# First expert's number from batch 0's routing, made inside the last attention step, with first-layer pieces in place of fillers

## The chip, the cores and the metric

One core of one Trainium2 chip runs the whole program. The metric is the device time of one execution in microseconds. Its engines work side by side, each through its own list of instructions in order: PE (matmuls, with PEld for the loads of weights), DVE, ACT and POOL (elementwise work and reductions), and SP, which only issues transfers here. An instruction that has to wait holds all that stand behind it in its engine's list.

## What is computed

Attention in two steps for 4 batches with 8 heads (576 positions, 64 channels, 32 packed queries `p`), then two mixture-of-experts layers with 8 experts.

```python
def sm_attn(qq, kk, vv):
    s = scale * np.matmul(qq, kk.transpose(0, 1, 3, 2))
    s = s - np.max(s, axis=-1, keepdims=True)
    a = np.exp(s)
    a = a / (np.sum(a, axis=-1, keepdims=True) + 1e-09)
    return np.matmul(a, vv)
p_packed = sm_attn(p, k, v)
out = sm_attn(q, p_packed, p_packed)

# first layer: x is [2304, 512]
logits = x @ w_gate
expert_idx = np.argmax(logits, axis=1)
...
h = np.maximum(np.einsum('ecd,edf->ecf', disp, w1), 0.0)   # the tokens kept for each expert
y = np.einsum('ecf,efd->ecd', h, w2)
out[i] = gate_w[i] * y[expert_idx[i], pos[i]]
# second layer: the same with its own weights, no capacity, and a second gate
```

All tokens of a batch go to one expert with these inputs. The kernel finds that expert on the chip, fetches its weights alone, and keeps a general path for other inputs, which is not run here.

## The kernel before

**Attention.** The loop over the batches is a pipeline written out by hand. `att_iter(b)` does the first scores of batch b, the packed values of b - 1 and the second softmax of b - 2, head groups 0 and 1 apart. `att_last` is the step of the last batch (n = 3, o = 2, r = 1), `att_end` what is left behind it (o = 3, r = 2, z = 1); the second softmax of batch 3 follows behind `att_end`. In the names of instructions: `tp` and `a1Tp` are transposes on PE, `T` and `a1T`, `a1L` their copies out of PSUM; `s` are scores; `nb` is the row maximum of the first softmax, `a` its exponential on ACT; `pp` is the packed value, `pps`, `ppTp` and `ppT` its scaled form, transpose and copy; `sT` is the second score, whose softmax goes DVE (`mx`, maximum), POOL (subtract), ACT (exponential), DVE (`dn`, one over the sum), POOL (multiply), DVE (L401, back to `a2T`).

**Routing of batch 0.** `g1_t(0, 1)` gives batch 0's logits `Lall` on DVE (L434). `ga` and `ga2` make the one-hot of the maximum: `mx`, `d`, `first`, `mx`, `oh` (L166 to L176). `gb` ranks the tokens on PE (`rk`), `gc` turns ranks into `kp` and `K`, the tokens within capacity (L465 to L470), `gd` counts `K` on PE (`cp`) and takes the expert with most tokens (`primary`, L205 to L212). L222 turns it into an integer, `e_i`. SP loads it into a register (L685) and uses it as the address of the weights: `moe1_load1` (eight transfers of 256 KB, L516) and `moe1_load2` (four of 512 KB, L529).

**First expert layer of batch 0.** Its matmuls are made of a high and a low half of each operand. `moe1_x` splits the input: `xh` on ACT (L538), `xl` on POOL (L539). The layer is cut into twelve pieces in the list `fill`: four `ppw` pieces (the packed values times a quarter of the weights, then `wh` on ACT and `wl` on DVE) and eight `h` pieces (twelve matmuls each, then ACT's high half L573 and DVE's low half L580). `FL(n)` places the next n of them wherever it stands. `att_end` has five places, each for one piece, and one `warm(4)`, four matmuls on zeros whose result nobody reads. The other seven pieces stand behind, among the second softmax of batch 3. Then the second-layer weights are split (`w2ah` on ACT, `w2al` on DVE, L498), and `y`, the second layer, begins. Inside the first `y` stands `lp`, the routing of batches 1 to 3, which needs the last `a2T`.

**PSUM.** All PE results share four buffers of PSUM (`psm`). A matmul that starts a new tile waits until the reader of the tile that held the buffer is done.

Of the kernel before, what the change touches and what calls it, by code (L numbers as in the profile page):

```python
# [11 lines left out]
I32 = mybir.dt.int32  # L12
ACTF = mybir.ActivationFunctionType
ALU = mybir.AluOpType
AX = mybir.AxisListType
# [13 lines left out]
def tile_kernel(  # L29
# [16 lines left out]
    nc = tc.nc  # L46
# [112 lines left out]
    def bc(ap, n):  # L159
        return ap.unsqueeze(2).to_broadcast([ap.shape[0], ap.shape[1], n])  # L160

    def onehot(L, nm, V=nc.vector):

        n = L.shape[1]
        mx = sm_p.tile([128, n], FP32, tag=nm + "mx", name="mx")
        nc.vector.tensor_reduce(mx, L, axis=AX.X, op=ALU.max)  # L166
        d = sm_p.tile([128, n, E], FP32, tag=nm + "d", name="d")
        V.tensor_tensor(d, L, bc(mx, E), op=ALU.subtract)
        first = sm_p.tile([128, n, E], FP32, tag=nm + "f", name="first")
        rv = revv.rearrange("p b t e -> p (b t) e")[:, 0:n, :]  # L170

        def rest():
            nc.vector.scalar_tensor_tensor(first, d, 0.0, rv, op0=ALU.is_equal, op1=ALU.mult)
            nc.vector.tensor_reduce(mx, first, axis=AX.X, op=ALU.max)
            oh = sm_p.tile([128, n, E], BF16, tag=nm + "oh", name="oh")
            nc.vector.tensor_tensor(  # L176
                oh, rev.unsqueeze(1).to_broadcast([128, n, E]), bc(mx, E), op=ALU.is_equal)
            return oh, d
        return rest

    def denom(ex, nm):
# [38 lines left out]
    def to_int(src, nm, V=nc.vector):  # L220
        t = keep_p.tile(list(src.shape), I32, name=nm)
        V.tensor_copy(t, src)  # L222
        return t
# [48 lines left out]
    def transp(b, nm, G, eng=0):  # L272

        src = raws.pop((nm, b, G))
        t = t_p.tile([128, J, 128], FP32, tag="T", name="T")
        for j0, n in ((0, 6), (6, 3)):
            ps = psm("tp")
            for j in range(n):
                tr(nc, ps[:, j // 3, (j % 3) * 128:(j % 3) * 128 + 128],
                   src[:, 2 * (j0 + j):2 * (j0 + j) + 2, :].rearrange("p r d -> p (r d)"), ident)  # L280
            evac(eng, t[:, j0:j0 + n, :].rearrange("x (u j) c -> x u (j c)", j=3), ps[:, 0:n // 3, 0:384])
        T[nm, b, G] = t
# [96 lines left out]
    def s2_max(b, G):  # L379
        mx = as_p.tile([128, 2 * NB2], FP32, tag=f"mx2{G}", name="mx2")  # L380
        nc.vector.tensor_reduce(mx, sv(b, G), axis=AX.X, op=ALU.max)
        at["mx", b, G] = mx
# [44 lines left out]
    def g1_t(b0, b1):  # L427
        tp = psm("lt")
        for j in range(3):
            tr(nc, tp[:, 0, j * 128:(j + 1) * 128], lgT[:, j * 128:(j + 1) * 128], ident)  # L430
        tv = tp[:, 0, 0:384].rearrange("p (j u g b e) -> p b j u e g", j=3, u=2, g=2, b=4)
        for b in range(b0, b1):
            for u, t in ((0, 0), (1, 2)):
                nc.vector.tensor_reduce(  # L434
                    Lall[:, b, t:t + 2 + u, :], tv[:, (b - 1) % 4, 0:2 + u, u], axis=AX.X, op=ALU.add)

    def ga(b0, b1, nm, V=nc.vector):
        L = Lall[:, b0:b1].rearrange("p b t e -> p (b t) e")
# [96 lines left out]
    def moe1_x(a2, lo_eng):  # L535
        xh = xs_p.tile([128, 2, S], FP32R, tag="xh", name="xh")
        xl = xs_p.tile([128, 2, S], FP32R, tag="xl", name="xl")
        nc.scalar.activation(out=xh, in_=a2, func=ACTF.Copy)  # L538
        lo_eng.tensor_tensor(xl, a2, xh.bitcast(FP32), op=ALU.subtract)  # L539
        return xh, xl  # L540
# [143 lines left out]
    def val(ap, hi):  # L684
        return nc.values_load(ap, engines=sp, min_val=0, max_val=hi)  # L685
# [184 lines left out]
    def warm(n):  # L870
        ps = psm("warm")
        for _ in range(n):
            mm(nc, ps[:, 0, 0:256], wz[:, 0:128], wz, True, True)

    with tc.manual_schedule():
# [56 lines left out]
        def att_last():  # L932

            n, o, r = B - 1, B - 2, B - 3
            a1_T(o, 0, 0)
            s2_max(r, 0)
            s2_sub(r, 0, nc.gpsimd)
            s1_mm(n, 0)
            g1_t(0, 1)
            transp(o, "q", 0)  # L940
            s2_max(r, 1)
            s2_sub(r, 1, nc.gpsimd)
            s1_max(n, 0)
            s1_exp(n, 0)
            a1_T(o, 1, 1)
            s2_exp(r, 0)
            pp_mm(o, 0)
            s1_mm(n, 1)
            s1_max(n, 1)
            rest = ga(0, 1, "a0", nc.gpsimd)  # L950
            s1_exp(n, 1)
            pp_mm(o, 1)
            pp_scale(o)
            ga2(0, rest, nc.gpsimd)
            transp(o, "q", 1)
            s2_exp(r, 1)
            pp_T(o)
            gb(0, 1)
            gc(0, 1, "a0")
            s2_sum(r, 0)  # L960
            s2_mul(r, 0, nc.gpsimd)
            a1_T(n, 0, 0)
            s2_mm(o, 0)
            g1_g(o)
            s2_tr(o, 0)
            st["rest0"] = gd(0, 1, "a0")
            st["e0"] = to_int(pe1[:, 0:1], "e0_i")
            s1_rs(n)
            s2_mm(o, 1)
            s2_back(r, 0)  # L970
            s2_tr(o, 1)
            st["h"] = new_h()
            st["x"] = moe1_x(a2T[:, 0], nc.gpsimd)

        def att_end():

            o, r, z = B - 1, B - 2, B - 3
            transp(o, "q", 0)
            s2_sum(z, 1)
            s2_mul(z, 1, nc.gpsimd)  # L980
            a1_T(o, 1, 0)
            pp_mm(o, 0)
            s2_max(r, 0)
            pp_mm(o, 1)
            s2_sub(r, 0, nc.gpsimd)
            transp(o, "q", 1)
            pp_scale(o)
            s2_exp(r, 0)
            warm(4)
            pp_T(o)  # L990
            s2_back(z, 1)
            s2_max(r, 1)
            FL()
            s2_sub(r, 1, nc.gpsimd)
            s2_exp(r, 1)
            s2_mm(o, 0)
            s2_tr(o, 0)
            s2_sum(r, 0)
            g1_g(o)
            FL()  # L1000
            s2_mul(r, 0, nc.gpsimd)
            FL()
            s2_back(r, 0)
            s2_sum(r, 1)
            s2_mul(r, 1, nc.gpsimd)
            FL()
            s2_mm(o, 1)
            s2_tr(o, 1)
            s2_back(r, 1)
            FL()  # L1010
# [19 lines left out]
        for b in range(B):  # L1030
# [12 lines left out]
                att_iter(b)  # L1043
            else:
                att_last()
        e0 = val(st["e0"][0:1, 0:1], E - 1)
        st["w1"] = moe1_load1(e0)
        w2s = moe1_load2(e0)


        for i in range(4):
# [179 lines left out]
```

## Time and profile before

| | |
|---|---|
| median of 3 runs (lowest to highest) | 271.77 us (270.22 to 272.42) |
| the profiled execution: its time, its span | 269.92 us, 268.2 us |
| busy in the span | PE 250.5, PEld 215.8, DVE 131.0, ACT 100.2, POOL 35.0 us |
| mean granted clock of PE | 0.976 |

The span is the time from the first to the last instruction of the profiled execution. The busy time is the sum over an engine's instructions; an engine that is busy for a small share of the span can still be the one that others wait for in one stretch of it. The granted clock is the share of full speed (2.4 GHz) that PE got; 0.50 is 1.2 GHz.

### The profile page before, as it was taken

Reading aid. Unit: us, or ns where it says so; the run is one execution under the profiler, and the core shown is the slowest. Engines: PE = TensorE matmul, PEld = TensorE weight load, DVE = VectorE, ACT = ScalarE, POOL = GpSimd, SP = SyncE. Lnnn points to the kernel's source line nnn. Section 1 sums busy time; section 2 is a strip of 40 time slices with the busy share of each in tenths; the row PEclk is TensorE's granted clock in tenths of the full one; section 3 lists DMA queues with packets and bytes.
Section 4 is the critical chain, followed back from the end, with each engine's and each line's share of the span. In section 5 each row is a group of like instructions: output and inputs, shape, how many; then the busy total and the mean of one; then the engine's idle time right before and its main releaser. Section 6 shows DMA issues by size and latency. Waiting matters only on the chain.

```text
span 268.2 us, 5617 instructions
## 1 busy us (share of the span) xinstructions
PE 250.5 (93%) x2281; PEld 215.8 (80%) x2281; DVE 131.0 (49%) x323; ACT 100.2 (37%) x165; POOL 35.0 (13%) x65
## 2 busy tenths in 40 slices
PE   8879989959989989999999999999999999999980
PEld 6647657627886979879999999998888999988860
DVE  0232877985996685278641245695030425611000
ACT  2856566723480410345430243263221414411110
POOL 5001333533350240000000000000020000002000
PEclk9997999977999999999999999999999999999997
DMA  6999999059720004985696034228121460001211
GB/s 243 373 300 282 354 312 298 13 121 213 222 77 2 0 0 158 221 204 185 158 256 227 21 87 129 78 79 233 43 60 42 126 227 2 0 0 43 60 42 48
DMA packets 32867, 37.14 MB, mean 138 GB/s; under 512 B 6336, under 2 KB 27456, under 8 KB 32832
## 3 DMA queue, kind: packets, MB, share of 16 engines
q1 hardware_dynamic: 32832, 36.69, 46.8%
q8 instruction: 20, 0.33, 0.5%
q14 instruction: 15, 0.12, 0.2%
HBM read 31.25 MB, written 4.72 MB: 134 GB/s over the span
## 4 chain that ended last, share of the span: by engine, by line
PE 76%; DVE 9%; DMA 6%; SPq 4%; issue 1%; POOL 1%; ACT 0%; ACTq 0%; DVEq 0%; POOLq 0%
PE h L21 25%; PE o L21 19%; PE y L21 18%; DMA r<-in_q_dram 4%; PE tp L25 3%; PE pp L21 2%; DMA wraw<-in_moe_w_dram 2%; PE s L21 2%; PE l L21 2%; PE lp L21 2%; PE ppw L21 1%; SPq L269 1%; PE a1Tp L25 1%; DVE dn L392 1%; DVE eq L208 1%
## 5 line engine op out<-in xcount | busy, mean ns | idle before, releaser
L21 PE MATMUL o<-w2bh,h 128*128 128x512 f32 x144 | 45.9, 391 | 0.0
L21 PE MATMUL y<-h,w2ah 128*128 128x288 f32 x256 | 44.7, 296 | 0.0
L21 PEld LDWEIGHTS y<-h,w2ah 128*128 128x128 f32 x256 | 37.6, 189 | 0.0
L580 DVE SCALAR_TENSOR_TENSOR h<-h 128x576 fp32r<-128x576 f32 (+3 forms) x64 | 25.8, 447 | 20.7 <-ACT h L573 20.7
L573 ACT ACTIVATE h<-h 128x576 fp32r<-128x576 f32 x32 | 20.4, 650 | 35.9 <-PE h L21 32.3
L21 PEld LDWEIGHTS o<-w2bh,h 128*128 128x128 f32 x144 | 26.9, 188 | 5.7
L21 PE MATMUL o<-w2bl,h 128*128 128x512 f32 x80 | 31.3, 391 | 0.0
L21 PE MATMUL y<-h,w2al 128*128 128x288 f32 x128 | 27.6, 297 | 0.8 <-DVE w2al L498 0.8
L21 PE MATMUL h<-yh,w1bh 128*128 128x288 f32 x128 | 27.5, 296 | 0.0
L21 PE MATMUL h<-yh,w1bl 128*128 128x288 f32 x128 | 27.4, 295 | 0.0
L21 PE MATMUL h<-yl,w1bh 128*128 128x288 f32 x128 | 27.3, 295 | 0.0
L241 ACT ACTIVATE T<-tp 128x768 f32<-128x768 f32 (+1 forms) x32 | 18.9, 650 | 11.4 <-PE tp L25 11.3
L679 POOL TENSOR_SCALAR osb<-osb,g 64x512 f32<-64x512 f32 x2 | 3.1, 1570 | 147.5 <-DVE osb L678 147.5
L21 PEld LDWEIGHTS y<-h,w2al 128*128 128x128 f32 x128 | 20.5, 189 | 1.5 <-DVE w2al L498 1.0
L25 PE MATMUL tp<-ident,r 128*128 128x128 f32 x144 | 19.6, 283 | 2.0 <-DMA r<-in_q_dram 1.9
L25 PEld LDWEIGHTS tp<-ident,r 128*128 128x128 f32 x144 | 16.4, 146 | 5.8 <-issue 2.4
L21 PEld LDWEIGHTS h<-yh,w1bh 128*128 128x128 f32 x128 | 20.6, 189 | 0.2
L21 PEld LDWEIGHTS h<-yh,w1bl 128*128 128x128 f32 x128 | 20.6, 188 | 0.0
L21 PEld LDWEIGHTS h<-yl,w1bh 128*128 128x128 f32 x128 | 20.6, 188 | 0.0
L589 ACT ACTIVATE yh<-y 128x576 fp32r<-128x576 f32 x8 | 5.2, 652 | 39.9 <-PE y L21 39.9
L671 ACT ACTIVATE osb<-o,g 128x512 f32<-128x512 f32 x8 | 5.5, 688 | 36.9 <-PE o L21 29.0
L590 DVE TENSOR_TENSOR yl<-y,yh 128x576 fp32r<-128x576 f32 x8 | 6.0, 755 | 25.7 <-ACT yh L589 25.7
(177 smaller groups left out, 378.3 us busy)
## 6 DMA issues: line engine op xcount, KB each, us to landing
wraw<-in_moe_w_dram SPq DMA_DIRECT2D x24, 512.0 KB, 5.5
r<-in_k_dram SPq DMA_DIRECT2D x8, 576.0 KB, 7.7
r<-in_q_dram SPq DMA_DIRECT2D x8, 576.0 KB, 9.6
v<-in_v_dram SPq DMA_DIRECT2D x8, 512.0 KB, 10.7
wraw<-in_moe_w_dram SPq DMA_DIRECT2D x16, 256.0 KB, 5.4
out_dram<-zt SPq DMA_DIRECT2D x2, 1152.0 KB, 7.6
out_dram<-osb SPq DMA_DIRECT2D x8, 256.0 KB, 2.0
a2s<-a2T SPq DMA_DIRECT2D x1, 576.0 KB, 3.6
```

The source lines that it names most:

```text
L21: return nc.tensor.matmul(out, lhsT=lhsT, rhs=rhs, start=start, stop=stop)
L25: return nc.tensor.transpose(out, in_, ident)
L208: nc.vector.scalar_tensor_tensor(eq, eq, 0.0, revv[0:1, 0, 0:n, :], op0=ALU.is_equal, op1=ALU.mult)
L241: nc.scalar.activation(out=o, in_=i, func=ACTF.Copy)
L269: nc.sync.dma_start(t, src[b, :, 128 * VR:].rearrange("h p d -> p h d"))
L392: nc.vector.tensor_reduce(dn, sv(b, G), axis=AX.X, op=ALU.add)
L573: nc.scalar.activation(out=hi, in_=ps[:, :, 0:HS], func=ACTF.Relu)
L580: nc.vector.scalar_tensor_tensor(o, i, 0.0, a.bitcast(FP32), op0=ALU.max, op1=ALU.subtract)
L589: nc.scalar.activation(out=half(y[0][:, c, :]), in_=ps[:, :, 0:HS], func=ACTF.Copy)
L590: nc.vector.tensor_tensor(half(y[1][:, c, :]), ps[:, :, 0:HS], half(y[0][:, c, :]).bitcast(FP32), op=ALU.subtract)
L671: nc.scalar.activation(out=o[:n], in_=ps[:n, 0, :], func=ACTF.Copy, scale=g2[:n, t:t + 1])
L679: nc.gpsimd.tensor_scalar(o[:n], o[:n], g2[:n, t:t + 1], None, op0=ALU.mult)
```

## The change

Batch 0's one-hot is begun right behind its logits, and the expert's number is taken from it: from the routing of batch 0's first token, not from the count of all. The integer is made there (L943), and the loads of the first-layer weights are issued there. `d` goes from POOL to DVE; `first` and the second `mx` go from the second half of the one-hot to its first half. `moe1_x` moves from the end of `att_last` up to behind `ga2`. `att_end` gets one more place for a piece, and two pieces instead of the four fillers. The second-layer weights are asked for at the same place in the code as before.

```diff
@@ onehot
-        V.tensor_tensor(d, L, bc(mx, E), op=ALU.subtract)
+        nc.vector.tensor_tensor(d, L, bc(mx, E), op=ALU.subtract)
         first = sm_p.tile([128, n, E], FP32, tag=nm + "f", name="first")
         rv = revv.rearrange("p b t e -> p (b t) e")[:, 0:n, :]
+        nc.vector.scalar_tensor_tensor(first, d, 0.0, rv, op0=ALU.is_equal, op1=ALU.mult)
+        nc.vector.tensor_reduce(mx, first, axis=AX.X, op=ALU.max)
 
         def rest():
-            nc.vector.scalar_tensor_tensor(first, d, 0.0, rv, op0=ALU.is_equal, op1=ALU.mult)
-            nc.vector.tensor_reduce(mx, first, axis=AX.X, op=ALU.max)
             oh = sm_p.tile([128, n, E], BF16, tag=nm + "oh", name="oh")
...
+        rest.mx = mx
         return rest
@@ att_last
             g1_t(0, 1)
+            rest = ga(0, 1, "a0")
+            e0_i = keep_p.tile([1, 1], I32, name="e0_i")
+            nc.vector.tensor_scalar(e0_i, rest.mx[0:1, 0:1], -1.0, float(E), op0=ALU.mult, op1=ALU.add)
+            st["e0"] = val(e0_i, E - 1)
+            st["w1"] = moe1_load1(st["e0"])
             transp(o, "q", 0)
...
             s1_max(n, 1)
-            rest = ga(0, 1, "a0", nc.gpsimd)
             s1_exp(n, 1)
             pp_mm(o, 1)
             pp_scale(o)
             ga2(0, rest, nc.gpsimd)
+            st["x"] = moe1_x(a2T[:, 0], nc.gpsimd)
             transp(o, "q", 1)
...
             st["rest0"] = gd(0, 1, "a0")
-            st["e0"] = to_int(pe1[:, 0:1], "e0_i")
...
             st["h"] = new_h()
-            st["x"] = moe1_x(a2T[:, 0], nc.gpsimd)
@@ att_end
             s2_max(r, 0)
+            FL()
             pp_mm(o, 1)
...
             s2_exp(r, 0)
-            warm(4)
+            FL(2)
             pp_T(o)
...
-        e0 = val(st["e0"][0:1, 0:1], E - 1)
-        st["w1"] = moe1_load1(e0)
-        w2s = moe1_load2(e0)
+        w2s = moe1_load2(st["e0"])
```

How the lists of instructions change at three places (line numbers after the change are higher by one from L180 on, and by six or more in `att_last` and behind it).

DVE in `att_last`, from batch 0's logits to the scaling of the packed values, before and then after:

```order
L434 TENSOR_REDUCE Lall<-lt 128x24
L381 TENSOR_REDUCE mx_824<-sT 128x18
L307 TENSOR_REDUCE nb<-s 128x1
L243 COPY a1T<-a1Tp 128x512
L243 COPY a1L<-a1Tp 64x128
L307 TENSOR_REDUCE nb<-s 128x1
L166 TENSOR_REDUCE mx<-Lall 128x5
L350 TENSOR_SCALAR pps<-pp,sm 128x128 x2
L173 SCALAR_TENSOR_TENSOR first<-d,revv 128x40
L174 TENSOR_REDUCE mx<-first 128x5
L176 TENSOR_TENSOR oh<-rev,mx 128x40
```

```order
L435 TENSOR_REDUCE Lall<-lt 128x24
L166 TENSOR_REDUCE mx<-Lall 128x5
L168 TENSOR_TENSOR d<-Lall,mx 128x40
L171 SCALAR_TENSOR_TENSOR first<-d,revv 128x40
L172 TENSOR_REDUCE mx<-first 128x5
L943 TENSOR_SCALAR e_i<-mx 1x1
L382 TENSOR_REDUCE mx_855<-sT 128x18
L308 TENSOR_REDUCE nb<-s 128x1
L244 COPY a1T<-a1Tp 128x512
L244 COPY a1L<-a1Tp 64x128
L308 TENSOR_REDUCE nb<-s 128x1
L351 TENSOR_SCALAR pps<-pp,sm 128x128 x2
```

Five instructions, from `mx` to `e_i`, now stand ahead of the maxima and copies of the softmax.

ACT a little later in `att_last`, before and then after (the first row is the exponential of the second head group):

```order
L314 ACTIVATE a_880,sm<-s,nb 128x9x32x2
L241 ACTIVATE T<-tp 128x768
L241 ACTIVATE T<-tp 128x384
L388 ACTIVATE sT<-sT 128x576
L241 ACTIVATE a1T<-a1Tp 128x512
L241 ACTIVATE a1L<-a1Tp 64x128
L538 ACTIVATE xh<-a2T 128x1152
```

```order
L315 ACTIVATE a_906,sm<-s,nb 128x9x32x2
L539 ACTIVATE xh<-a2T 128x1152
L242 ACTIVATE T<-tp 128x768
L242 ACTIVATE T<-tp 128x384
L389 ACTIVATE sT<-sT 128x576
L242 ACTIVATE a1T<-a1Tp 128x512
L242 ACTIVATE a1L<-a1Tp 64x128
```

`xh` moved ahead of five other instructions; `xl` on POOL waits for it alone. On PE the place of `cp` and of the scores behind it is the same, but the scores now use a PSUM buffer that DVE frees with `gsz` (L414 before), where they waited for PE and ACT:

```order
L21 LDWEIGHTS ones16_89 [waits DVE_49]
L21 MATMUL cp_979<-K16_941,ones16_89 128x40 [waits PE_49]
L21 MATMUL s_995<-T_911,ppT_124 32x288 [waits PE_49,Activation_49]
L21 MATMUL s_995<-T_911,ppT_124 32x288 x7
L25 MATMUL tp_1043<-ident_84,r_548 128x128 [waits DMAHW0_49,DVE_49]
```

```order
L21 LDWEIGHTS ones16_89 [waits DVE_49]
L21 MATMUL cp_1007<-K16_969,ones16_89 128x40 [waits Activation_49]
L21 MATMUL s_1021<-T_939,ppT_124 32x288 [waits DVE_49]
L21 MATMUL s_1021<-T_939,ppT_124 32x288 x7
L25 MATMUL tp_1043<-ident_84,r_548 128x128 [waits DMAHW0_49,Activation_49]
```

DVE at the end of the stretch, in front of the second layer, before and then after:

```order
L556 TENSOR_TENSOR wl<-ppw,wh 128x512
L392 TENSOR_REDUCE dn_1320<-sT 128x18
L393 TENSOR_SCALAR dn_1320<-dn_1320 128x18
L394 RECIPROCAL dn_1320<-dn_1320 128x18
L392 TENSOR_REDUCE dn_1326<-sT 128x18
L393 TENSOR_SCALAR dn_1326<-dn_1326 128x18
L394 RECIPROCAL dn_1326<-dn_1326 128x18
L580 SCALAR_TENSOR_TENSOR h<-h 128x576
L498 TENSOR_TENSOR w2al<-wraw,w2ah 128x1024 x2
L401 STREAM_TRANSPOSE a2T<-sT 128x9x32x2
L580 SCALAR_TENSOR_TENSOR h<-h 128x576 x2
L401 STREAM_TRANSPOSE a2T<-sT 128x9x32x2
```

```order
L382 TENSOR_REDUCE mx_1326<-sT 128x18
L581 SCALAR_TENSOR_TENSOR h<-h 128x576 x2
L393 TENSOR_REDUCE dn_1360<-sT 128x18
L394 TENSOR_SCALAR dn_1360<-dn_1360 128x18
L395 RECIPROCAL dn_1360<-dn_1360 128x18
L393 TENSOR_REDUCE dn_1366<-sT 128x18
L394 TENSOR_SCALAR dn_1366<-dn_1366 128x18
L395 RECIPROCAL dn_1366<-dn_1366 128x18
L581 SCALAR_TENSOR_TENSOR h<-h 128x576
L499 TENSOR_TENSOR w2al<-wraw,w2ah 128x1024 x2
L402 STREAM_TRANSPOSE a2T<-sT 128x9x32x2 x2
```

The last three low halves of `h` stood behind `w2al` (two of them in the rows shown, one just behind); now all eight stand ahead of it.

## Rows read from the trace of the kernel before

**Rows 1.** Busy time by engine, mean granted clock, DMA share, GB/s, three windows.

```profile
core 0: us, PE busy (x) PEld busy (x) DVE busy (x) ACT busy (x) POOL busy (x), PEclk, DMA share, GB/s
42.30:54.30 12.00, 11.68 (x279) 8.77 (x278) 10.91 (x32) 8.68 (x17) 5.85 (x6) 1.00 0.41 112
54.30:66.50 12.20, 8.75 (x94) 5.31 (x92) 8.64 (x19) 4.29 (x7) 4.59 (x4) 0.72 0.86 174
66.50:85.00 18.50, 17.74 (x164) 15.37 (x165) 17.94 (x28) 8.59 (x13) 5.81 (x5) 1.00 0.39 115
```

**Rows 2.** Chain that ended last: start us, us, what (four `h` pieces in the last).

```profile
54.11 0.12 DVE e_i L222
...
57.66 5.12 DMA wraw<-in_moe_w_dram
...
123.68 6.58 PE h L21 x48
```

**Rows 3.** PE in time: start, us, line, operation, xcount [idle before <-releaser].

```profile
49.42 0.72 PE L21 MATMUL s<-T,ppT 64*32 64x288 f32 x16
...
56.12 0.60 PE L21 MATMUL warm<-wz 128*128 128x256 bf16 x4 [1.36 <-DVE sT L371]
58.22 0.66 PE L25 MATMUL ppTp<-ident,pps 128*128 128x128 f32 x2 [1.50 <-DVE pps L350]
59.20 1.85 PE L21 MATMUL ppw<-wraw,ppT 64*32 64x256 f32 x9 [0.33 <-DMA wraw<-in_moe_w_dram]
...
80.29 0.52 PE L21 MATMUL y<-h,w2al 128*128 128x288 f32 x2 [0.76 <-DVE w2al L498]
```

**Rows 4.** Busy time in windows of one microsecond, columns as in rows 1.

```profile
57.00:58.00 1.00, 0.00 (x0) 0.00 (x0) 1.00 (x4) 0.00 (x0) 0.71 (x1) 0.61 0.87 273
...
64.00:65.00 1.00, 1.00 (x8) 1.00 (x9) 0.93 (x5) 0.60 (x1) 0.12 (x1) 0.97 1.12 220
```

**Rows 5.** DVE in time, columns as in rows 3.

```profile
42.09 0.30 DVE L434 TENSOR_REDUCE Lall<-lt 128x16 f32<-128x32 f32 x2 [0.63 <-PE lt L25]
...
45.18 0.76 DVE L307 TENSOR_REDUCE nb<-s 128x1 f32<-128x576 f32 x1 [0.64 <-PE s L21]
...
48.09 0.23 DVE L468 TENSOR_SCALAR kp<-kp,capf 128x5 f32<-128x5 f32 x1
48.36 0.20 DVE L470 TENSOR_TENSOR K<-oh,kp 128x40 bf16<-128x40 bf16 x1
...
49.65 0.12 DVE L414 COPY gsz<-gp 128x16 f32<-128x16 f32 x1
...
51.09 2.60 DVE L208 SCALAR_TENSOR_TENSOR eq<-eq,revv 1x8 f32<-1x8 f32 x1
...
57.12 0.69 DVE L381 TENSOR_REDUCE mx<-sT 128x18 f32<-128x576 f32 x1
...
58.91 0.42 DVE L360 COPY ppT<-ppTp 128x256 f32<-128x256 f32 x1 [0.59 <-PE ppTp L25]
...
62.21 0.69 DVE L556 TENSOR_TENSOR wl<-ppw,wh 128x512 fp32r<-128x512 f32 x1 [1.55 <-ACT wh L555]
...
66.52 0.76 DVE L580 SCALAR_TENSOR_TENSOR h<-h 128x576 fp32r<-128x576 f32 x1 [1.16 <-ACT h L573]
...
78.38 3.00 DVE L498 TENSOR_TENSOR w2al<-wraw,w2ah 128x1024 fp32r<-128x1024 f32 x2
...
81.99 1.38 DVE L580 SCALAR_TENSOR_TENSOR h<-h 128x576 fp32r<-128x576 f32 x2
```

**Rows 6.** ACT and POOL in time, columns as in rows 3.

```profile
46.03 0.80 ACT L314 ACTIVATE a<-s,nb 128x576 f32<-128x576 f32 x1 [0.71 <-DVE nb L307]
...
49.27 1.16 ACT L538 ACTIVATE xh<-a2T 128x1152 fp32r<-128x1152 f32 x1
...
51.00 2.67 POOL L539 TENSOR_TENSOR xl<-a2T,xh 128x1152 fp32r<-128x1152 f32 x1
...
58.40 1.16 POOL L385 TENSOR_TENSOR sT<-sT,mx 128x576 f32<-128x576 f32 x1
```

**Rows 7.** DVE in time, routing of batches 1 to 3, under POOL's `w2al`.

```profile
94.52 2.39 DVE L470 TENSOR_TENSOR K<-oh,kp 128x120 bf16<-128x120 bf16 x1
```

## Prediction

> **What bounds the kernel now.** I read the busy time of the stretch that the change touches first, 42.3 to 85 us, in three windows [rows 1]. PE is nearly full in the first and the last (11.68 of 12.00, 17.74 of 18.50) but has 8.75 of 12.20 in the middle, at a mean granted clock of 0.72. The chain of waits says why: the expert's number e_i is ready at 54.11 + 0.12 = 54.2, and the weights fetched by it are the last thing waited for until 57.66 + 5.12 = 62.8 [rows 2]. PE in order of time shows the hole: waits of 1.36, 1.50 and 0.33 us between 54.8 and 59.2 [rows 3]. One-microsecond windows then show the clock at half (1.2 GHz) from inside 57:58 (0.61, so from about 57.2) to the start of 64:65 (0.97, so to about 64.1) [rows 4]. Waits of 3.2 us and work at half clock: that is what the change fills.
>
> DVE is the other half of the picture. It has 10.91 of 12.00 in the first window and 17.94 of 18.50 in the last [rows 1]. Between them its own idle pieces are 0.59, 1.55 and 1.16, all waits for PE or ACT [rows 5]. At the end of the stretch it is PE that waits: y is held 0.76, until 80.29, by DVE's w2al (low half of the second-layer weights) [rows 3, 5]. So the two engines take turns, and a gain on PE is kept only if DVE gets to w2al earlier too.
>
> **The change, part by part.**
>
> *Weights.* e_i is now made right behind batch 0's logits, which DVE has at 42.09 + 0.30 = 42.4 [rows 5]. Five small DVE instructions that wait for each other, 0.20 to 0.23 each like kp and K [rows 5], some 1.2 in all: e_i at 43.6, 10.6 earlier. From the number to the fourth of the eight transfers it took 8.6 (54.2 to 62.8); that would be 52.2. Attention's own loads are ahead in the queues: DMA is 0.41 busy over 42.3:54.3, 4.9 us, so until about 48 [rows 1]. A transfer of 256 KB at 220 GB/s is 1.2 us [rows 4]: first pair near 51, fourth near 53, last near 58. PE asks for the first pair at 55 or later (below) and for each next one several microseconds after. So the transfers are hidden, by attention's matmuls; a pair that came late would cost its own 2.4.
>
> *The five instructions in front.* They stand ahead of mx, both nb and the copies of a1T. 1.2 late, of which DVE waited 0.64 anyway before the second nb [rows 5], and two of them no longer come later. Left on DVE at the end of this list: +0.3 (bounds 0 and 0.5). PE's second pp waits for a1L and, with it, pps and kp: about +0.5 there.
>
> *xh and xl moved up.* This is the term that decides. xh (1.16 on ACT) now stands right behind the second group's exponential, which started at 46.03 and now starts near 46.4; with 0.80 and its accumulator read it ends near 47.2, xh near 48.4. So POOL's xl (2.67) runs from 48.4 to 51.1 instead of 51.00 to 53.67 [rows 6]. Before, xl held DVE's tiny L208 for 2.60, until xl had ended [rows 5, 6]; K of the later batches is held 2.39 in the same way under POOL's w2al [rows 7]. Now DVE reaches kp at 48.09 + 0.5 = 48.6, inside xl, so kp or K is held and K ends near 51.4 instead of 48.56. DVE loses the 2.4 that it lost before, only earlier. But behind L208 no matmul waited for DVE; behind K stands PE's cp, and gsz, whose PSUM tile the following s now takes. gsz came 1.29 behind K (48.36 and 49.65) [rows 5], so that s starts near 52.8 instead of 49.42 [rows 3]. PE stands still for some 3.2 us from 49.6 with cp alone in it. The hole is moved, not closed.
>
> The Trainium skill (SBUF — State Buffer, Who interferes with whom) says that the pair of ports which VectorE and GpSimd share is taken for a whole instruction by whichever issues first, and the other one blocks. By it K is not held if it is issued before xl, and xl waits instead: the second rival.
>
> *The pieces.* Eight pieces instead of five stand in the end of attention, three of them (a ppw and two h) newly ahead of the last s. PE's work is the same less four fillers, 0.60 [rows 3]. Before, PE went from this s at 49.42 to 54.8 without a wait: 5.3. With ppw0 (an estimate of 0.6, by the s of as many matmuls, 0.72) it is near 58.7, and then waits for wl0, which DVE does behind mx. wl1 hangs on ACT behind an exponential, and that on POOL's subtraction (1.16) behind mx [rows 6]: mx ends near 58.3, the subtraction, which waits for another one, near 60.3, the exponential 61.0, wh1 61.5. DVE idles some 1.9 there. From 59.2 PE does two ppw, four h (6.58 for four [rows 2]), ppTp, s and gp, 9.2 with estimates of 0.6, 0.2, 0.7 and 0.2 for the small ones: the last s near 68.5, and then ppw3 and four h, 7.2, to about 76.
>
> *DVE up to w2al.* Here the sum is made, from the end of mx (57.12 + 0.69) to that of w2al (78.38 + 3.00 = 81.4) [rows 5]. The instructions are the same, but three low halves of h that stood behind w2al now stand ahead of it: 1.38 for two, so 3 x 0.69 = +2.1. Idle before 0.59 + 1.55 + 1.16 = 3.3, after 1.9 and an estimate of 0.3 for small waits: -1.1. Late at the start: +0.3. Sum **+1.3**: w2al is ready at 82.7, its first half (1.1 earlier) at 81.6.
>
> *Clock.* PE's waits up to 59.20 brought the clock to half, and it rose 4.9 after work resumed [rows 3, 4]. The hole from 49.6 to 52.8 is as long. At half until 4.9 behind it PE would lose 2.4, at full nothing; but PE waits for wl0 and wl1 there anyway: **+0.5**. In front of y: PE is through with h near 76, and y cannot go on before 81.6, 5.6 us with four matmuls in it, where 0.76 stood. If the clock falls, y goes on at half, and PE alone sets the time from there. Bounds 0 (the 0.76 left the clock alone) and 2.4 (half of 4.9); the wait is nearer to the second: **+1.6**.
>
> Sum 1.3 + 0.5 + 1.6 = **+3.4 us**. The profiled execution took 269.92, 1.85 under the median of the runs shown, 271.77; it would take 273.3. On the median I expect 271.77 + 3.4 = **275.2 us**.
>
> **The rivals.**
>
> 1. *DVE is late, but the clock holds.* The wait in front of y may be cut up by y's first matmuls and a late h piece. For it: 0.76 at y left the clock alone. Against: 1.36, 1.50 and 0.33 with work between them did not. 271.77 + 1.3 = 273.1. Chance 0.27.
>
> 2. *K is issued ahead of xl.* By my count K meets xl by only 0.5 us. Then cp runs near 49.5 and the lock falls on the small steps behind K; gsz still comes near 51.4, so 1.4 of PE's stall goes, and with it the first 0.5 and an estimate of 0.4 of the 1.3. With the clock's 1.6 at y full or absent this is +0.9 to +2.5, in the middle 273.5. Chance 0.10.
>
> 3. *PE alone is the bound: faster.* Place: from 54.8 to y. The waits of 3.2 and 0.76 vanish, and half of the 4.9 us that PE worked at half clock, 2.4: -6.4, less the new stall's part, 2.4: -4.0, so 267.8. It decides if w2al is ready before 77.4 (81.4 - 4.0), so if DVE closes its 3.3 of idle and the three low halves cost it nothing. For it: the chain before y runs through the wait for the weights [rows 2]. Against: DVE's 17.94 of 18.50. Chance 0.15.
>
> **How the numbers follow.** About 1% (2.7 us) is what a measurement of this kernel can tell from no change. The forecast, 273.5 to 277.5 by itself and nearly all of it above 274.5, has 0.48: slower. Rivals 1 and 2 are within 1%: 0.37. Rival 3 is faster: 0.15. The range takes in rivals 1 and 2 and goes up to 1.3 + 2.4 + 2.4 = 6.1 and an estimate of 0.6 for PE's slack, so 278.5; down it goes to 270.5, where only rival 3 is left out.
>
> **What would show each step.** Weights: e_i near 43.6, no wait of PE for a transfer. Lock: xl near 48.4 to 51.1, a kp or K of over 2 us, cp at 51 or later, s near 52.8. DVE: three h rows ahead of w2al, which ends near 82.7. Clock: PE idle 2 us or more in front of y, and half clock on y's first matmuls. I am wrong if w2al ends before 80, if kp and K take 0.2 each, or if the clock stays full in 80:86.

## The result, and the profile after

The changed kernel takes 274.87 us (median; 273.28 to 276.54), the kernel before beside it 271.22: a ratio of 1.0141 (95% interval 1.0096 to 1.0186), so it is slower by 3.65 us. The profiled execution took 273.28 us, its span is 271.6.

The three windows of [rows 1], and the stretch from batch 0's logits to the start of `w2al` (same columns):

```profile
42.30:54.30 12.00, 8.55 (x179) 6.06 (x178) 11.02 (x32) 6.68 (x13) 5.15 (x4) 0.91 1.09 232
54.30:66.50 12.20, 11.57 (x212) 9.20 (x211) 8.96 (x17) 6.63 (x12) 3.44 (x3) 0.95 0.50 129
66.50:85.00 18.50, 14.00 (x115) 12.79 (x114) 17.30 (x30) 8.19 (x13) 6.95 (x6) 0.85 0.16 54
41.43:79.86 38.43, 31.75 (x497) 25.68 (x495) 33.72 (x78) 21.66 (x37) 15.45 (x14) 0.95 0.60 147
```

The hole of the middle window is filled (PE 11.57 of 12.20, before 8.75), but the first window has lost 3.1 us of PE's work and the last one 3.7. DVE (third pair of numbers) is about as full as before at both ends (11.02, before 10.91; 17.30, before 17.94). DVE and POOL in time, then PE:

```profile
41.43 0.31 DVE L435 TENSOR_REDUCE Lall<-lt 128x16 f32<-128x32 f32 x2 [0.63 <-PE lt L25]
42.70 0.14 DVE L943 TENSOR_SCALAR e_i<-mx 1x1 int32<-1x1 f32 x1
47.73 2.65 POOL L540 TENSOR_TENSOR xl<-a2T,xh 128x1152 fp32r<-128x1152 f32 x1 [0.70 <-ACT xh L539]
47.90 2.50 DVE L469 TENSOR_SCALAR kp<-kp,capf 128x5 f32<-128x5 f32 x1
50.44 0.20 DVE L471 TENSOR_TENSOR K<-oh,kp 128x40 bf16<-128x40 bf16 x1
57.93 0.69 DVE L557 TENSOR_TENSOR wl<-ppw,wh 128x512 fp32r<-128x512 f32 x1 [0.67 <-ACT wh L556]
61.12 0.69 DVE L557 TENSOR_TENSOR wl<-ppw,wh 128x512 fp32r<-128x512 f32 x1 [1.98 <-ACT wh L556]
62.23 0.76 DVE L581 SCALAR_TENSOR_TENSOR h<-h 128x576 fp32r<-128x576 f32 x1 [0.41 <-ACT h L574]
79.86 2.98 DVE L499 TENSOR_TENSOR w2al<-wraw,w2ah 128x1024 fp32r<-128x1024 f32 x2
...
50.69 0.19 PE L21 MATMUL cp<-K,ones 128*128 128x40 bf16 x1 [1.56 <-DVE K L471]
51.89 1.01 PE L21 MATMUL s<-T,ppT 64*32 64x288 f32 x16 [1.01 <-DVE gsz L415]
78.75 0.79 PE L21 MATMUL y<-h,w2ah 128*128 128x288 f32 x4 [2.29 <-ACT w2ah L498]
81.76 0.85 PE L21 MATMUL y<-h,w2al 128*128 128x288 f32 x2 [2.22 <-DVE w2al L499]
...
87.17 3.51 PE L21 MATMUL lp<-a2T,gsz 128*32 128x320 f32 x24
```

No wait of PE for a weight transfer is left ([rows 3] had 0.33, and the chain 5.12 in [rows 2]). `xl` holds `kp` for 2.50, PE stands still in front of `cp` and `s`, DVE waits 1.98 for the second `wh`, and in front of `y` there are waits of 2.29 and 2.22 where 0.76 stood. The clock in windows of one microsecond (it stands third from the end):

```profile
52.00:53.00 1.00, 1.00 (x17) 0.25 (x16) 0.93 (x4) 0.00 (x0) 1.00 (x1) 0.59 1.15 239
55.00:56.00 1.00, 1.00 (x18) 0.78 (x20) 1.00 (x2) 0.65 (x3) 0.00 (x0) 0.70 0.88 178
79.00:80.00 1.00, 0.55 (x4) 0.31 (x3) 0.97 (x4) 0.65 (x1) 0.53 (x1) 0.75 0.00 0
86.00:87.00 1.00, 1.00 (x8) 1.00 (x7) 0.00 (x0) 0.00 (x0) 0.00 (x0) 0.84 0.00 0
```

It is 0.50 in every microsecond between the first two rows and between the last two: half from 52.2 to 55.6, and from 79.5 to 86.3 on the first of `y`. The half clock of 57 to 64 [rows 4] is gone; a shorter one has come behind the waits of `cp` and `s`, and a new one at `y`.

**A ruler for all kernels here.** From `lp` to the end every profile has the same time: 268.2 - 83.67 = 184.5 before, 271.6 - 87.17 = 184.4 after, 184.3 to 184.6 in the rest. The time in front of batch 0's logits varies by chance, 41.4 to 45.0 us, in part with attention's own loads (in `fill`, the latest, PE waits about 6 us for them up to there, in the changed kernel 3.1). So each edit is read from three numbers of the stretch between: DVE's busy time from the start of `Lall` to the start of `w2al`, DVE's idle time there (length less busy), and from there to `lp` (5.3 at full clock).

| kernel | median us | ratio, 95% interval | DVE busy | DVE idle | `w2al` to `lp` | sum |
|---|---|---|---|---|---|---|
| before | 271.22 | 1 | 31.38 | 4.91 | 5.29 | 41.58 |
| changed | 274.87 | 1.0141 (1.0096 to 1.0186) | 33.72 | 4.71 | 7.31 | 45.74 |
| x_back | 273.97 | 1.0103 (1.0059 to 1.0147) | 33.84 | 4.74 | 7.48 | 46.06 |
| order | 271.92 | 1.0026 (0.9996 to 1.0055) | 31.79 | 5.43 | 6.12 | 43.34 |
| fill | 273.21 | 1.0044 (1.0015 to 1.0072) | 33.70 | 4.57 | 5.29 | 43.56 |
| weights | 268.04 | 0.9876 (0.9833 to 0.9919) | 31.75 | 2.50 | 5.30 | 39.55 |
| xl_early | 268.71 | 0.9889 (0.9848 to 0.9930) | 31.61 | 3.98 | 5.30 | 40.89 |
| xl_dve | 267.23 | 0.9833 (0.9792 to 0.9874) | 30.59 | 2.53 | 5.30 | 38.42 |
| no_fill | 269.55 | 0.9938 (0.9907 to 0.9969) | 31.75 | 3.84 | 5.28 | 40.87 |
| before_fill | 271.18 | 1.0010 (0.9976 to 1.0043) | 31.48 | 5.01 | 5.29 | 41.78 |
| p_first | 271.75 | 1.0008 (0.9968 to 1.0047) | 31.79 | 4.23 | 6.82 | 42.84 |
| p_second | 272.59 | 1.0079 (1.0042 to 1.0115) | 31.80 | 6.31 | 5.29 | 43.40 |
| late_w2 | 271.76 | 1.0011 (0.9976 to 1.0047) | 33.90 | 2.65 | 6.19 | 42.74 |
| p_swap | 269.12 | 0.9902 (0.9864 to 0.9941) | 31.87 | 3.21 | 5.30 | 40.38 |

Each set of experiments had its own runs of the kernel before beside it (medians of 270.6 to 271.7), so ratios are compared, not medians. The last four columns come from one profiled execution each, and need not agree with the medians: `weights` is 2.0 us under the kernel before in the sum and 3.4 by the ratio.

### The profile page after: what moved, and what is told of

It is laid out like the page before. It is cut to its first block, busy times and chain, and to the rows that moved or that the text cites. A ratio compares the mean times of both kernels' runs of the same rounds, so it can differ in the third digit from the quotient of the medians.

```text
span 271.6 us, 5608 instructions
## 1 busy us (share of the span) xinstructions
PE 248.5 (91%) x2277; PEld 216.1 (80%) x2277; DVE 131.4 (48%) x324; ACT 100.5 (37%) x165; POOL 34.7 (13%) x64
## 4 chain that ended last, share of the span: by engine, by line
PE 76%; DVE 10%; DMA 7%; SPq 1%; issue 1%; POOL 1%; ACT 1%; ACTq 0%; DVEq 0%; POOLq 0%
PE h L21 26%; PE o L21 19%; PE y L21 18%; DMA r<-in_q_dram 6%; PE tp L25 4%; PE pp L21 2%; PE l L21 2%; DVE h L581 2%; PE lp L21 2%; PE ppw L21 1%; DMA r<-in_k_dram 1%; DVE kp L469 1%; SPq L270 1%; DVE dn L393 1%; DVE K L471 1%
## 5 line engine op out<-in xcount | busy, mean ns | idle before, releaser
L21 PE MATMUL y<-h,w2ah 128*128 128x288 f32 x256 | 46.2, 304 | 2.3 <-ACT w2ah L498 2.3
L21 PEld LDWEIGHTS y<-h,w2ah 128*128 128x128 f32 x256 | 38.9, 195 | 2.5 <-ACT w2ah L498 2.5
L21 PE MATMUL y<-h,w2al 128*128 128x288 f32 x128 | 28.5, 305 | 2.2 <-DVE w2al L499 2.2
L21 PEld LDWEIGHTS y<-h,w2al 128*128 128x128 f32 x128 | 21.4, 196 | 3.0 <-DVE w2al L499 2.4
```

What stands on the lines that cost most here:

```text
L21: return nc.tensor.matmul(out, lhsT=lhsT, rhs=rhs, start=start, stop=stop)
```

## The experiments

The theory was the prediction's: the early weights are hidden and gain little, `xl`'s lock moves a hole, three low halves in front of `w2al` make DVE late, and the clock falls in front of `y`. The rivals are told with each.

### Parts of the change undone: x_back, order, fill

`x_back` puts the input's split back:

```diff
-            st["x"] = moe1_x(a2T[:, 0], nc.gpsimd)     # behind ga2
...
             st["h"] = new_h()
+            st["x"] = moe1_x(a2T[:, 0], nc.gpsimd)
```

> The change, but with the input's split (`xh`, `xl`) back at its old place at the end of `att_last`; all else as changed. Theory (the lock moves a hole, and DVE in front of `w2al` sets the end): `kp` and `K` take 0.2 to 0.3 each, `cp` runs near 49.5 and the next `s` near 50, so PE's waits of 1.56 and 1.01 us go and the clock does not fall in 52 to 56; DVE's small `L208` is held by `xl` instead. PE then waits for `wl` in 55 to 61 instead, and `w2al` still ends within 0.5 us of 82.84: 274.3 to 275.1 us, at most 0.6 under the changed kernel. Rival (the hole in front of 52 is what the change costs): the 2.6 us of waits and the half clock behind them come off the end: 271.8 to 272.6 us.

The waits in front of `cp` and `s` went, `kp` took 0.23, and the small instruction at L209 was held instead, as the one at L208 in [rows 5]:

```profile
51.24 2.60 DVE L209 SCALAR_TENSOR_TENSOR eq<-eq,revv 1x8 f32<-1x8 f32 x1
56.16 0.55 PE L25 MATMUL tp<-ident,r 128*128 128x128 f32 x3 [1.23 <-DVE sT L372]
58.51 0.67 PE L21 MATMUL ppw<-wraw,ppT 64*32 64x256 f32 x16 [1.80 <-DVE wl L557]
82.26 0.85 PE L21 MATMUL y<-h,w2al 128*128 128x288 f32 x2 [2.21 <-DVE w2al L499]
```

PE waits for DVE at 56.16 (1.23) and 58.51 (1.80) instead, and the clock falls there (half from 59.9 to 63.3). DVE's idle time is 4.74 against 4.71. Measured 273.97; its interval overlaps that of the changed kernel, and the rival's 271.8 to 272.6 lies below it in ratio (1.0059 to 1.0147 of 271.4 is 273.0 to 275.4). The hole at 49 to 52 is not by itself what the change costs: with it closed, waits as long and a half clock as long (3.4 us) come a little later.

`order` lets three `h` pieces stand behind `w2al` again:

```diff
         s2_sub(b, 1, nc.gpsimd)
-        FL(2)
         s2_exp(b, 0)
...
         s2_mul(b, 1, nc.gpsimd)
-        FL()
         ws = [split(w, "w2a", i, nc.vector) for i, w in enumerate(w2s[:2])]
```

> The change, but with three pieces fewer between the second softmax of batch 3 and the split of the second-layer weights, so that three `h` pieces stand behind `w2al` as before the change. Theory (DVE's order, with the clock that hangs on it): the three low halves, 2.1 us, leave the way of `w2al`, which is ready near 80.7; the wait of PE in front of `y` falls under 1 us and the clock stays full behind it: 1.5 to 2.1 us from DVE and 1.5 to 2.3 from the clock, so 270.8 to 272.0 us. If only the DVE term is real and the clock falls all the same: 273.0 us. Rival (the low halves only change places, `y` waits for them instead of for `w2al`): 274.5 to 275.0 us.

271.92: the theory's range. In the profile both parts are smaller than it had them. DVE's work ahead of `w2al` fell by 33.72 - 31.79 = 1.93, of which its idle time gave back 0.7, so that `w2al` starts 1.2 earlier behind the logits; from there to `lp` another 1.2 comes off. The wait for `w2al` in front of `y` is 0.95; the half clock behind it is shorter (81.2 to 84.6, in place of 79.5 to 86.3) but not gone, and `w2ah` is still waited for:

```profile
78.97 0.79 PE L21 MATMUL y<-h,w2ah 128*128 128x288 f32 x4 [1.75 <-ACT w2ah L498]
80.72 0.53 PE L21 MATMUL y<-h,w2al 128*128 128x288 f32 x2 [0.95 <-DVE w2al L499]
```

`fill` works the waits in front of `y` away with matmuls on zeros:

```diff
-        moe1_layer2(st["h"], ws, 0, y0, {14: logits, 18: onehots})
+        warm(14)
+        moe1_layer2(st["h"], ws, 0, y0, {2: lambda: warm(14), 14: logits, 18: onehots})
```

> The change, with 14 matmuls on zeros (2.1 us at full clock) in front of the first `y` and 14 more behind its first two matmul pairs, in the two waits of 2.29 and 2.22 us; they wait for nothing that DVE does. Theory (the half clock behind the waits costs by itself): DVE is untouched, `w2al` still ends near 82.8, but the clock stays full from 79 to 87; PE worked there at half for some 4.6 us behind 81.76, of which 2.3 come off: 272.4 to 273.3 us. Rival (DVE alone sets the end there, the clock only fills time in which PE would wait): 274.5 to 275.2 us.

273.21, the theory's range. DVE is the same (33.70 busy, 4.57 idle); the clock is full from the first `y` to `lp`, and `w2al` to `lp` takes 5.29 in place of 7.31. So the clock alone costs 2.0 us there. (Batch 0's logits come 3.6 later in this profile than in that of the changed kernel.)

```profile
82.16 0.78 PE L21 MATMUL y<-h,w2ah 128*128 128x288 f32 x4 [0.75 <-ACT w2ah L498]
85.16 0.53 PE L21 MATMUL y<-h,w2al 128*128 128x288 f32 x2 [0.68 <-DVE w2al L499]
```

From the first `y` to `lp`, clock third from the end:

```profile
82.16:88.54 6.38, 5.71 (x42) 5.05 (x42) 5.40 (x7) 0.90 (x1) 1.39 (x2) 1.00 0.01 3
```

### The early weights alone: weights, before_fill, no_fill

`weights` is the changed kernel with `moe1_x`, the five places of `att_end` and the four fillers as before:

```diff
             s2_max(r, 0)
-            FL()
             pp_mm(o, 1)
...
             s2_exp(r, 0)
-            FL(2)
+            warm(4)
             pp_T(o)
```

> The kernel before with the early number and the early loads of the first-layer weights alone: the input's split, the five places for pieces and the four fillers as before. Theory (the fetch was the last thing waited for only by a little, DVE stands close behind): PE's wait of 0.33 for the first transfer and the later ones go, the two DVE waits of 1.36 and 1.50 in front stay and so does the half clock behind them; 270.6 to 271.8 us, no more than 1.2 under the kernel before. Rival (the fetch bounds the stretch, and the two waits and the clock go with it): 267.5 to 269.5 us.

268.04, the rival's range: the theory fell. The two waits of [rows 3] are still there, but the clock stays full throughout, and DVE's idle time is halved, 2.50 against 4.91. The stretch from the logits to `w2al`, columns as in [rows 1]:

```profile
41.87:76.12 34.25, 29.75 (x494) 23.91 (x493) 31.75 (x74) 20.16 (x35) 15.42 (x14) 1.00 0.64 158
```

PE in time:

```profile
56.25 0.60 PE L21 MATMUL warm<-wz 128*128 128x256 bf16 x4 [1.30 <-DVE sT L372]
58.35 0.49 PE L25 MATMUL ppTp<-ident,pps 128*128 128x128 f32 x2 [1.50 <-DVE pps L351]
78.03 0.53 PE L21 MATMUL y<-h,w2al 128*128 128x288 f32 x2 [0.75 <-DVE w2al L499]
```

Is that gain the fetch or the clock? `no_fill` has the early weights without the fillers (the line `warm(4)` taken out):

> The kernel with the early number and loads alone (268.0 us), without its four fillers near 56 us. There PE then stands still 3.4 us (1.30 + 0.60 + 1.50) without work. Theory (the half clock in 57 to 64 of the kernel before comes of PE's waits there, and the fillers with the first weights in time just keep it off): the clock falls to half for 3 to 5 us behind the wait, and 1.0 to 2.4 us are lost: 269.0 to 270.4 us. Rival (it came of the late weights alone): the clock stays full, 267.8 to 268.3 us.

PE in time, and a window of one microsecond (columns as in [rows 1]):

```profile
59.15 0.73 PE L25 MATMUL ppTp<-ident,pps 128*128 128x128 f32 x2 [3.30 <-DVE pps L351]
```

```profile
58.00:59.00 1.00, 0.00 (x0) 0.00 (x0) 1.00 (x3) 0.00 (x0) 0.69 (x1) 0.65 0.00 0
```

The timeline shows one wait of 3.30, the window of 58 to 59 the fall: half clock from 58.3 to 65.1, longer than the 3 to 5 us expected, and 269.55, in the expected range. DVE, which does the same work, idles 1.34 more. `before_fill` is the other way round, twelve fillers in the kernel before (`warm(4)` to `warm(12)`):

> The kernel before, with twelve fillers in place of four near 56 us, so that PE works until about 57.9 of the 58.2 at which the next work is ready; the number and the weights come as late as before. Theory (the early weights gained both ways: a third from the fetch itself, the rest because the clock stays full): the half clock in 57 to 64 goes or shrinks, PE still waits for the later transfers, which land until 63: 269.8 to 270.6 us. Rival 1 (all of the gain was the clock): 268.0 to 268.8 us. Rival 2 (all was the fetch): 271.2 to 271.8 us.

271.18, no gain (1.0010, 0.9976 to 1.0043): the theory's 269.8 to 270.6 fell, though only by a little, and rival 2 has the number. PE's wait for `pps` shrank to 0.63, but behind it the late transfers are waited for and the clock falls all the same, later and shorter (60.5 to 63.9):

```profile
57.82 0.50 PE L25 MATMUL ppTp<-ident,pps 128*128 128x128 f32 x2 [0.63 <-DVE pps L350]
58.90 0.62 PE L21 MATMUL ppw<-wraw,ppT 64*32 64x256 f32 x2 [0.58 <-DMA wraw<-in_moe_w_dram]
60.14 0.44 PE L21 MATMUL ppw<-wraw,ppT 64*32 64x256 f32 x7 [0.62 <-DMA wraw<-in_moe_w_dram]
```

In the sums: before 41.58, early weights at half clock (no_fill) 40.87, at full clock (weights) 39.55. So of the 2.0 us 0.7 came with the clock at half and 1.3 with the clock full; by the ratios (0.9938 and 0.9876) it is 1.7 and 1.7. Neither early weights without fillers nor more fillers with late weights kept the clock full; the two together did. That the late fetch is what brought the clock down in the kernel before is not shown: the clock had fallen there at 57.2 [rows 4], and PE's first wait for a transfer is the 0.33 in front of 59.20 [rows 3].

### The lock: xl_early, xl_dve

`xl_early` is `weights` with `moe1_x` behind `ga2` as in the change:

> The kernel with the early number and loads alone (268.0 us), and in it the input's split moved up behind `ga2` as in the change; the pieces and the four fillers as before. Theory (the lock moves a hole that costs little, since PE waits for DVE anyway a little later): `kp` is held about 2.5 us, PE waits some 1.5 and 1.0 in front of `cp` and `s`, and DVE, which loses 2.4 at `kp` in place of 2.4 at `L209`, starts `w2al` 34.0 to 34.8 us behind batch 0's logits (34.25 without the move): 267.8 to 269.0 us. Rival (the hole costs what it measures, with the half clock behind it): 2.6 to 3.5 more, 270.6 to 271.6 us.

```profile
50.05 2.50 DVE L469 TENSOR_SCALAR kp<-kp,capf 128x5 f32<-128x5 f32 x1
54.04 1.22 PE L21 MATMUL s<-T,ppT 64*32 64x288 f32 x16 [0.98 <-DVE gsz L415]
```

268.71, in the theory's range; its interval overlaps that of `weights`. In its profile, which is its slowest run (270.67), the clock is half from 52.6 to 59.4, DVE idles 1.48 more, and `w2al` starts 35.59 behind the logits, later than the theory's 34.0 to 34.8. By the medians and this one sum the move costs between 0 and 1.3 us. That it is the clock is likely (the mean granted clock of this run is 0.972, of the other five 0.979 to 0.989) but not shown: the faster runs have no profile.

`xl_dve` is `weights` with `moe1_x(a2T[:, 0], nc.vector)` at the old place:

> The kernel with the early number and loads alone (268.0 us), with `xl` computed by DVE in place of POOL, at the old place. Theory (POOL's long instruction holds DVE's small ones, and DVE sets when `w2al` is ready): DVE pays 1.36 for `xl` itself, and `L208` and `L209` take 0.3 and 0.15 instead of up to 2.6, so DVE is some 1.0 earlier and `w2al` starts 33.0 to 33.5 us behind batch 0's logits: 266.7 to 267.4 us. Rival 1 (PE sets the time between 52 and 78, DVE's wait was cover): 267.7 to 268.4 us. Rival 2 (1.36 more on DVE holds `mx` and the copies for PE): 268.6 to 269.4 us.

```profile
53.16 0.15 DVE L209 SCALAR_TENSOR_TENSOR eq<-eq,revv 1x8 f32<-1x8 f32 x1
55.50 1.31 DVE L540 TENSOR_TENSOR xl<-a2T,xh 128x1152 fp32r<-128x1152 f32 x1
```

267.23, the lowest median here, 1.7% under the kernel before (0.9792 to 0.9874). Its interval overlaps that of `weights`, so the 0.8 us between the two medians are not clear of noise; DVE's rows show the mechanism. L209 takes 0.15 in place of 2.60, `xl` 1.31: DVE's busy time falls by 1.16 and the sum by 1.13. The Trainium skill (Perfetto Trace Analysis, Optimizing Scalar/DVE Operations) says that moving operations between GPSIMD and DVE might not help, since they share a port. This trace shows where it does: the lock costs DVE more time (2.60) than the work itself (1.31).

### The pieces: p_first, p_second, p_swap, late_w2

`weights` and `x_back` differ by the added places for pieces and the fillers alone, and by 6.5 in the sum. `p_first` and `p_second` add one of the places to `weights` and take one piece from the `FL(2)` behind `att_end`.

```diff
             s2_max(r, 0)
+            FL()          # p_first
             pp_mm(o, 1)
...
             s2_exp(r, 0)
             warm(4)
+            FL()          # p_second
             pp_T(o)
```

> The kernel with the early number and loads alone (268.0 us), and in it one of the three added places alone: the first `ppw` ahead of the second `pp`, and one piece fewer in the double place behind `att_end`, so that as many pieces as before stand ahead of `w2al`. Theory (what the added pieces cost beside the three low halves is DVE's wait for a `wl` whose `wh` stands behind an exponential on ACT): this `wh` stands ahead of the exponential, `wl` waits little, `w2al` starts 34.2 to 34.8 us behind batch 0's logits: 267.8 to 268.8 us. Rival (any piece that goes in between attention's steps delays its maxima and scores by its own length, 0.6 us and 0.7 us of copies, for each of the three): 269.3 to 270.3 us.

271.75, above both ranges. No `wh` is waited for, as the theory had it, but PE waits 1.80 in front of the fillers for `wl`, which stands behind `mx` on DVE and reads the PSUM buffer of this `ppw`:

```profile
54.96 0.66 PE L21 MATMUL ppw<-wraw,ppT 64*32 64x256 f32 x14 [0.34 <-DMA wraw<-in_moe_w_dram]
59.83 0.60 PE L21 MATMUL warm<-wz 128*128 128x256 bf16 x4 [1.80 <-DVE wl L557]
```

The early weights are not quite early enough for this place: the `ppw`, begun 10.9 us behind the logits, waits 0.34 for a transfer. The clock falls behind the wait of 1.80 (61.0 to 64.4), DVE idles 1.73 more, and the clock falls again behind waits of 0.82 and 0.92 in front of `y`: 6.82 to `lp`.

> The same with the second place in place of the first: the first `ppw` behind the fillers and behind the exponential `s2_exp` in ACT's list, one piece fewer behind `att_end`. Theory (`wh` has to wait for that exponential, which waits for POOL's subtraction behind DVE's `mx`; DVE holds at `wl` meanwhile): DVE idles some 2 us at `wl`, `w2al` starts 36.0 to 36.8 us behind the logits, and with a fall of the clock behind PE's wait 2.0 to 4.0 are lost: 270.0 to 272.0 us. Rival (the place is as good as the first): 267.8 to 268.8 us.

272.59; the mechanism is the theory's, its size was put too low (`w2al` starts 38.11 behind the logits, 36.0 to 36.8 expected). ACT, DVE and PE in time:

```profile
59.27 0.68 ACT L389 ACTIVATE sT<-sT 128x576 f32<-128x576 f32 x1 [3.87 <-POOL sT L386]
59.86 1.07 ACT L556 ACTIVATE wh<-ppw 128x512 fp32r<-128x512 f32 x2
...
60.47 0.69 DVE L557 TENSOR_TENSOR wl<-ppw,wh 128x512 fp32r<-128x512 f32 x1 [2.46 <-ACT wh L556]
...
61.64 0.72 PE L21 MATMUL s<-T,ppT 64*32 64x288 f32 x16 [2.66 <-DVE ppT L361]
```

`ppw` was done at 57.0, but `wh` stands behind the exponential `sT`, which waits for POOL's subtraction. DVE's `wl` waits for `wh`, the copy `ppT` stands behind `wl`, and PE's `s` waits for `ppT`; the clock is half behind that wait, from 62.7 to 66.1. `p_swap` moves the one line:

```diff
-            s2_exp(r, 0)
             warm(4)
             FL()
+            s2_exp(r, 0)
             pp_T(o)
```

> The kernel with the first `ppw` at the second place, with one line moved: `s2_exp(r, 0)` stands behind the fillers and the piece, so that on ACT `wh` no longer stands behind an exponential that waits for POOL; the matmuls are in the same order. Theory (DVE's 2.46 us of wait for `wh` near 58 to 60.5, and PE's 2.66 behind it, come of ACT's order alone): `wh` runs near 57, the wait goes, `w2al` starts 35.3 to 36.3 us behind the logits in place of 38.11 (the three low halves play no part here), and 1.8 to 3.5 come off 272.6: 269.1 to 270.8 us. Rival (the piece itself between attention's steps, its PSUM buffer held until `wl`, delays the rest wherever `wh` stands): 271.8 to 272.8 us.

269.12, ratio 0.9902 where `p_second` had 1.0079. `wh` runs at 58.23, ahead of the exponential, DVE's idle time falls from 6.31 to 3.21, and the sum by 3.02, although the clock is still half from 58.9 to 62.3:

```profile
58.23 0.60 ACT L556 ACTIVATE wh<-ppw 128x512 fp32r<-128x512 f32 x1 [1.68 <-PE ppw L21]
60.40 0.68 ACT L389 ACTIVATE sT<-sT 128x576 f32<-128x576 f32 x1 [1.58 <-POOL sT L386]
```

`late_w2` is `weights` with the last `FL()` ahead of the split made `FL(4)`: three more `h` pieces there, no other moved.

> The kernel with the early number and loads alone (268.0 us), with the last three `h` pieces ahead of the split of the second-layer weights, as many as in the change; no other piece moved. Theory (the three low halves are 2.07 us of DVE's work in front of `w2al`, and `y` waits for it): `w2al` starts 35.9 to 36.5 us behind the logits (34.25 without), PE waits over 2 us in front of `y`; 1.3 to 2.1 us if the clock holds, and 2.0 more if it falls as in the changed kernel: 269.3 to 272.0 us, the middle 270.7. Rival (the low halves only change places, the end is the same): 267.8 to 268.5 us.

271.76, in the theory's range. DVE is 33.90 busy, 2.15 more than in `weights`, and the clock falls behind a wait of 1.68 in front of `y` (half from 82.2 to 85.6; 6.19 to `lp`). The low halves do not just change places.

## Why the prediction came out as it did

I predicted 275.2 us, 270.5 to 278.5, slower the likeliest; it took 274.87. Times in the table are from the start of `Lall` (42.09 before, 41.43 after), so that the two profiles can be laid side by side.

| step | predicted | measured |
|---|---|---|
| `e_i` ready | 1.5 | 1.41 |
| weights hidden | no wait of PE for a transfer | none |
| `xl` | 6.3 to 9.0, `kp` or `K` held | 6.30 to 8.95, `kp` held 2.50 |
| `cp`, next `s` | 8.9, 10.7 | 9.26, 10.46 |
| DVE's wait for the second `wh` | 1.9, by way of POOL | 1.98, by way of PE |
| last `s`, last `h` piece done | 26.4, 33.9 | 27.3, 35.0 |
| `w2al` ready, against before | +1.3 | 82.84 - 41.43 = 41.41, +2.1 |
| clock at the first hole | +0.5 | not told apart: DVE idle 4.71 with the hole and half clock behind it, 4.74 in `x_back` with half clock as long elsewhere |
| clock in front of `y` | +1.6 | 7.31 - 5.29 = +2.0 |
| sum | +3.4 | +4.16 in this stretch, +3.65 in the medians |

**Right.** The lock, the three low halves (DVE's busy time rose by 2.34, predicted +2.1 and +0.3), the wait in front of `y` and the half clock on it. `order` and `late_w2` show the low halves (1.93 and 2.15 of DVE's work), `fill` the clock on `y` (2.0). The lock agrees with the page cited there (SBUF — State Buffer, Who interferes with whom, of the Trainium skill): a `tensor_scalar` on 128 x 5 numbers was held 2.50 by a POOL instruction that ran across it.

**Right in size, wrong in mechanism.** The prediction has the second `wh` wait for an exponential, and that for POOL's subtraction. ACT and POOL in the changed kernel:

```profile
57.91 1.16 POOL L386 TENSOR_TENSOR sT<-sT,mx 128x576 f32<-128x576 f32 x1
58.84 1.19 ACT L242 ACTIVATE T<-tp 128x768 f32<-128x768 f32 x2 [0.94 <-PE tp L25]
59.92 0.69 ACT L389 ACTIVATE sT<-sT 128x576 f32<-128x576 f32 x1
60.49 0.60 ACT L556 ACTIVATE wh<-ppw 128x512 fp32r<-128x512 f32 x1
```

The subtraction was done at 59.07 and nothing waited for it. The exponential followed the copies `T`, and these had waited for PE's transposes. PE was late, out of the lock's hole and the half clock behind it, and worked from 51.89 to 64.8 with no wait listed, where the prediction had it wait for both `wl`. So the reason for taking only 0.5 for the clock there ("PE waits for wl0 and wl1 there anyway") failed too. By these rows the exponential ahead of `wh` makes up at most 0.6 of the 1.98 (from 59.92 to 60.49). That 1.9 and 1.98 agree is luck. In `x_back` ACT does wait for that subtraction (2.40), and DVE's wait is 1.87.

Two readings behind the prediction were wrong as well. The prediction says that "behind L208 no matmul waited for DVE"; but PE's wait of 1.36 in [rows 3] is for `sT`, which DVE has behind L208 in its list, and in `xl_dve`, where that instruction is not held, no wait for `sT` is listed. So the lock had cost PE a hole at its old place too, which fits how little `x_back` and `xl_early` change. And the waits up to 59.20 did not all bring the clock to half: it was there at 57.2. (PE's 9.2 from 59.2 on adds up to 8.9 from its own terms.)

**Mis-sized.** The term -1.1 in the sum for `w2al` (idle 3.3 before, 1.9 and 0.3 after). DVE idled 0.67 + 1.98 + 0.41 = 3.06 there, and over the stretch 4.71 against 4.91: -0.2. I counted one late `wh` and left 0.3 for the rest, but the first `wl` and the first `h` waited too, for ACT's halves, for which ACT had waited 0.60 and 0.45 for PE's `ppw` and `h`. The term for the clock at `y` was 0.4 too little; the 0.5 at the first hole has no row of its own. The stretch grew by 4.16, not 3.4. That the median came within 0.4 us of the forecast is in part luck: the kernel before, too, measured 0.55 lower (271.22) than the 271.77 that the forecast started from.

**Not seen.** I sized the change as one. Its first half alone gives what rival 3 put on the whole: 268.04, against 267.8. Rival 3's condition (`w2al` ready before 77.4) was not met there: it is ready 37.24 behind the logits, 79.3 on the scale of before. But DVE's idle time fell by 2.4, 1.3 of it with the clock (`no_fill` against `weights`); I had taken 1.1, and that with all the rest of the change. From `weights` to the changed kernel the sum grows by 6.19: 1.97 of DVE's work (low halves), 2.21 of DVE's idle time and 2.01 of clock behind `y`. How much of the idle time hangs on the one line `s2_exp` in the changed kernel itself was not tried; for one piece alone it is 3.1 (`p_second` to `p_swap`), in the changed kernel by the rows above at most 0.6. What the rest of the 2.21 comes of is argued from these rows, not shown by a run. Why `p_first` loses at `y` too stays open.

## What to carry to other kernels

Size each part of a change by itself: an early fetch that gains 1.2% can be buried under a reordering made to use it. When a piece is put into a gap of one engine, follow its results through the in-order lists of the others: a copy that lands behind an instruction which waits on a third engine stalls everything behind it, and one line moved can be worth 3 us (`p_second` to `p_swap`). Count a long POOL instruction by what it holds up on DVE and, behind that, on PE.

## What the runs showed of the hardware that I had not expected

The fall of the clock cannot be told from the length of a wait. Waits of 1.30 and 1.50 with 0.60 of fillers between left it full (`weights`); 1.36 and 1.50 with the same fillers between did not, and the clock was half from 57.2, inside the second wait [rows 3, 4]. A single wait of 1.77 left it full (`xl_dve`). Waits of 1.29 and 0.91, with the same matmuls between, came with half clock from 58.9 in `p_swap`, inside the second; in `p_second` the clock stayed full through them and fell only behind a third wait, of 2.66. In front of `y`, 0.82 and 0.92 were followed by half clock in `p_first`, 0.83 and 0.92 in `p_second` were not. The rows, of `xl_dve`, `p_first` and `p_second`:

```profile
59.00 0.49 PE L25 MATMUL ppTp<-ident,pps 128*128 128x128 f32 x2 [1.77 <-DVE pps L351]
...
81.05 0.53 PE L21 MATMUL y<-h,w2al 128*128 128x288 f32 x2 [0.92 <-DVE w2al L499]
...
81.44 0.53 PE L21 MATMUL y<-h,w2al 128*128 128x288 f32 x2 [0.92 <-DVE w2al L499]
```

The kernels differ in what stands ahead, and these rows do not say which difference counts.

The time to batch 0's logits, with no edit ahead of it, ran from 41.4 to 45.0 us over the profiled runs. That is as much as most effects measured here, and why the stretch behind it was the better ruler.
